# Loading v and z as fp32 through SyncE's queue, with casts by ScalarE and GpSimd, in a fused attention and token-mixing kernel

## The chip, the cores and the metric

The kernel runs on one core of a Trainium2 chip. The time is the device time of one execution in microseconds (us). Of the kernel before, three runs are shown: 773.23, 775.76 and 777.05 us, median 775.76.

Names: PE is TensorE (PEld its weight loads), DVE is VectorE, ACT is ScalarE, POOL is GpSimd, SP is SyncE. The letter q after an engine's name means its instruction queue.

## The reference

All inputs and the output are fp32; u, v have the shape [8, 3200, 256], z has [8, 3200, 64].

```
scores = (1 / 3200) * z @ z.T            # per batch, 3200 x 3200
attn   = max(scores, 0) ** 2
x      = u * (attn @ v)                  # [8, 3200, 256]

wq, wk = x @ w_q, x @ w_k                # [8, 3200, 64]
W      = (1 / 8) * wq @ wk.T             # per batch, 3200 x 3200
out    = max(W @ x, 0) @ w_out           # [8, 3200, 256]
```

## The kernel before

**Tiling.** The 3200 rows of a batch are 25 tiles of 128, in seven groups of columns: six of 512 and one of 128. For every group the kernel makes score tiles (a 128-row tile of z against the group's columns), squares their positive part, and adds the products with v into accumulators. Two score tiles form a pair: they sit in the two halves of the PE array's rows and share one PSUM slot of two banks. There are two such slots.

**Stages of a pair.** `scores` (L263, PE) writes `sc` in PSUM. `first_stage` evicts it as max(4s, 0) into an fp32 tile `g`, on ACT (L286) or DVE (L290). `second_stage` squares it into an fp16 tile `at`, on ACT (L306) or POOL (L308). The pool of `g` has 7 buffers, that of `at` 16. The score matrix is symmetric, so part of the `at` blocks is not made a second time but turned: SP issues a DMA transpose from `at` to `tt` or `ttl` (L330).

**Second product.** `second_product` (L351, PE) multiplies blocks of `at` or `tt` with rows of `v_sb`, the fp16 copy of v, into `acc`. One step of it is two matmuls, on the two halves of the rows. There are 5,000 such steps in all. At the end of half a group, `gate` adds the two accumulators (L368 on ACT or DVE, L369 on DVE) and POOL multiplies by u (L388) into `x_sb`.

**The second layer.** `x_sb` is transposed by DMA (L400), projected to queries and keys (L417, evicted at L431), the keys are transposed by DMA (L436) and doubled by POOL (L448), and heads = keys.T @ x are summed over the groups (L455, L470). When a batch's heads are known, `mix` (L483) and `proj` (L521) give the output of that batch, evicted by ACT (L551) or DVE (L546) and stored by SP (L552). This work of batch b runs inside the loop of batch b + 1.

**Loads.** u comes by SP as fp32 (L174). v and z of the next batch come as DMAs that cast fp32 to fp16 on the way; these are issued by POOL: `load_v` (L150) five times a batch with 5 row tiles each, `load_z` (L156) once a batch. v has two buffers `v_sb`, so the next batch's v is written while this one's is read. z lands in `zn`, and SP transposes it into `zT` in four DMAs (`turn_z`, L163). The first batch's z is loaded as fp32 and cast on three engines (L110, L124); its v comes by casting DMAs of POOL (L113).

**The order.** All engines run in the order in which the Python program writes the instructions; each engine waits in that order for its operands. The order comes from a planner in the program: it keeps a clock for PE, DVE, ACT and POOL, adds a cost for each instruction (`give`), and chooses the engine of an eviction or a square by these clocks. SP's DMAs stand in a list `moves` with a time when they are ready, a time when they are due, SP's issue cost and the time that the DMA queue takes; `send` issues the one that is due first and plans its landing. A block of `tt` is due 4, 9 or 12 us after its square, by the distance of the groups. `at_time` puts an action at a planned time. `lead` is how many steps of the second product the scores are ahead of the even pace. `SPARE`, `BIAS` and `LATE` bend the choice between engines, `MIXES` spaces the output work, and `calm_for` keeps other work away from the end of a half group.

In every batch but the last, `batch_begun` plans the loads of the next: z 6 us after the batch begins, z's transposes 14 us later and on, v at 20, 33, 46, 59 and 72 us. Of these casting DMAs only the landing is planned (`v_at`); nothing on ACT or POOL waits for it.

Of the kernel before, what the change touches and what calls it, by code (L numbers as in the profile page):

```python
# [16 lines left out]
def kernel(  # L17
# [128 lines left out]

    def load_v(b, n0, nn):
        if n0 == 0:
            vs[b] = pv.tile([P, NT, D], FP16, tag="v_sb", name="v_sb")
        nc.gpsimd.dma_start(out=vs[b][:, n0 : n0 + nn, :], in_=rows(v, b)[:, n0 : n0 + nn, :])  # L150

    ztimes = []
    ZTURNS = [(0, 0, 7), (1, 0, 7), (0, 7, 13), (1, 7, 13)]

    def load_z(b):
        nc.gpsimd.dma_start(out=zn[:, 1 : NT + 1, :], in_=rows(z, b))  # L156

# [441 lines left out]
    mixed_at = []  # L599
    MIXES = 10.0  # L600
    MIXES_END = 14.0
# [7 lines left out]
    LANDS = 4.0  # L609
    RING = 2.0  # L610
    SLACK = 1.0

    def at_time(t, fn):
        later.append((t, fn))
# [80 lines left out]
    def squares():  # L695
        while pending and pending[0][0] <= clock[PE] + 0.3:
# [9 lines left out]
            for (b, gi, gj, _, nn, _, _), turn in second_stage(p, g, ways):  # L706
                n = nn * widths[gi] // P
                due = done + {1: 4.0, 2: 9.0}.get(gj - gi, FARDUE)
                out_of[p] = out_of.get(p, 0) + 1
                move(  # L710
                    done + SLACK, due + SLACK, 1.28, 0.21 * n, turn,
                    lambda t, x=(p, b, gi, gj, nn): block_landed(t, *x),
                    lambda x=(b, gi, gj): has_home(*x),
                )
# [17 lines left out]
    def use_keys(b, gi):  # L732
# [17 lines left out]
        if not final:  # L750
            move(
                done + SLACK, done + 10.0, 1.28, 0.21 * n, lambda: turn_keys(b, gi),
                lambda t: at_time(t, lambda: double(b, gi)),
            )
            keyed.append((b, gi))
# [61 lines left out]
    def project_out(b, gi, ps, ready):  # L817
        stores = []
        on_act = max(clock[ACT], ready) + BIAS <= max(clock[DVE], ready) + 0.2
        proj_out(b, gi, ps, [(not on_act, nc.sync, widths[gi] // P)], stores)  # L820
        engine, t = (ACT, 1.0) if on_act else (DVE, 1.23)
        done = give(engine, ready, t if gi < LASTG else 0.3)
        close_slot(done)
        i = len(stored)
        if gi < LASTG:
            stored.append(1e9)

        def landed(t):
            if gi < LASTG:
                stored[i] = t  # L830

        move(done + SLACK, done + 6.0, 0.55, 1.6, stores[0], landed)

    def push(takes):
        give(POOL, clock[PE], 0.6)
        dma_at[0] = max(dma_at[0], clock[PE]) + takes

    Z0 = 24
    ZWAIT, ZDUE, ZSTEP, ZSTEP0 = 14.0, 32.0, 7.0, 5.0
    V0 = 56  # L840
    V1 = 10

    def batch_begun(b, t):
        if b + 1 < B:
            t0 = max(t + 6, Z0)
            at_time(t0, lambda: (load_z(b + 1), push(3.0)))
            step = ZSTEP if b else ZSTEP0
            for i, (_, m0, m1) in enumerate(ZTURNS):
                move(
                    t0 + ZWAIT + step * i, t0 + ZDUE + step * i, 1.28, 0.21 * (m1 - m0),  # L850
                    lambda i=i: turn_z(b + 1, i),
                    lambda t, i=i: z_ready.update({(b + 1, i): t}),
                )
            for i in range(5):
                at = t + 20 + 13 * i if b else V0 + V1 * i
                at_time(at, lambda i=i: v_loaded(b + 1, 5 * i, 5))

    def v_loaded(b, n0, nn):
        load_v(b, n0, nn)
        push(2.5)  # L860
        for n in range(n0, n0 + nn):
            v_at[b, n] = dma_at[0] + 5.0

# [6 lines left out]
    def group_begun(b, gi, t):  # L870
        if gi == 0:
            batch_begun(b, t)
        if gi + 1 < NG:
            move(max(t + 2, clock[POOL] + SLACK), t + 7, 0.55, 1.6, lambda: load_u(b, gi + 1))
        elif b + 1 < B:
            move(max(t + 2, clock[POOL] + SLACK), t + 7, 0.55, 1.6, lambda: load_u(b + 1, 0))

    SPARE = 0.5
    BIAS = 0.2
    XDUE = 5.0  # L880
    XWAIT = 2.0
    LATE = 0.5

    def half_done(b, gi, half):
# [10 lines left out]
        if half == halves(gi)[-1]:  # L895
            n = 8 if widths[gi] == W else 2
            move(
                t + SLACK, t + XDUE, 1.28, 0.21 * n, lambda: turn_x(b, gi),
                lambda t: x_landed(t, b, gi), lambda: len(xTs) < NXT,
# [120 lines left out]
    at_time(V3, lambda: (load_first_v(4, 8), give(POOL, clock[PE], 0.6)))  # L1020
    move(10.0, 14.0, 0.55, 1.6, lambda: load_u(0, 0))
    load_weights()
# [3 lines left out]
    done_acc = 0  # L1026
    lead = 140
    turn_about = False
# [146 lines left out]
```

## Time and profile before

One execution was profiled. It took 773.15 us; its span, from the first instruction to the last, is 770.9 us.

| What | us | share of the span |
|---|---|---|
| Profiled execution, its own time | 773.15 | |
| Its span | 770.9 | |
| PE busy | 761.7 | 99% |
| POOL busy | 591.1 | 77% |
| ACT busy | 561.2 | 73% |
| DVE busy | 510.5 | 66% |
| DMA queue of SP, share of the 16 DMA engines | | 85.0% |
| DMA queue of POOL, share of the 16 DMA engines | | 14.8% |

Issuing a DMA counts as busy on POOL (0.59 us each) but not on SP. Matmul rows overlap, since a matmul starts before the one ahead of it has ended; so the mean of a matmul's row is longer than its step. In rows of groups, the order is: line, engine, operation, output<-inputs, shapes, count, then busy us and mean ns of one, then the idle time before them and what ended it. In rows of one source line the durations are minimum/median/maximum in ns.

### The profile page before, as it was taken

To read this page: it belongs to the slowest core of one execution; us is meant where nothing else is said; L and a number is where in the kernel's file an instruction comes from. 1 tells how busy PE (TensorE), PEld (TensorE's weight loads), DVE (VectorE), ACT (ScalarE), POOL (GpSimd) and SP (SyncE) were. 2 spreads that over 40 slices of the span, in tenths; PEclk is the share of its full clock that TensorE was granted. 3 is DMA by queue.
4 is the path that set the end of the run, shared out by engine and by line. 5 is a ranking of instruction groups with operands and counts; after the bars stand their busy time and mean duration, and the time that the engine had idled before them with its cause. 6 is when DMAs were issued, how large, how long until landed. Compare 5 with 4: busy or idle time off the path is not lost.

```text
span 770.9 us, 28221 instructions
## 1 busy us (share of the span) xinstructions
PE 761.7 (99%) x12408; PEld 678.4 (88%) x12408; DVE 510.5 (66%) x537; ACT 561.2 (73%) x647; POOL 591.1 (77%) x496
## 2 busy tenths in 40 slices
PE   8999999999999999999999999999999999999996
PEld 7889998888898888989889988998889989898884
DVE  6775876675787566765677756765667476675645
ACT  7785876778758678875788677877777676777734
POOL 8796788789687778666778687887878887888740
PEclk9999999999999999999999999999999999999998
DMA  8999999999999999999899999999999998979625
GB/s 199 130 187 182 167 204 173 160 212 194 194 162 189 194 209 190 182 213 203 153 190 162 188 231 163 219 145 160 262 156 192 184 190 211 201 143 203 152 84 191
DMA packets 307114, 141.09 MB, mean 183 GB/s; under 512 B 285744, under 2 KB 288432, under 8 KB 306992
## 3 DMA queue, kind: packets, MB, share of 16 engines
q1 hardware_dynamic: 300224, 123.13, 85.0%
q0 software_dynamic: 6624, 15.98, 14.8%
q8 instruction: 97, 1.59, 0.9%
q14 instruction: 25, 0.20, 0.1%
q10 hardware_dynamic: 144, 0.20, 0.1%
HBM read 59.64 MB, written 26.21 MB: 111 GB/s over the span
## 4 chain that ended last, share of the span: by engine, by line
PE 94%; POOL 2%; DVE 1%; DMA 1%; ACT 1%; issue 1%; POOLq 0%; SPq 0%; DVEq 0%; ACTq 0%
PE acc L351 68%; PE sc L263 13%; PE fo L521 6%; PE qk L417 3%; PE qk L455 2%; POOL at L308 2%; PE mx L483 1%; DMA z<-in_z_dram 1%; POOL x_sb L388 1%; DVE g L290 0%; ACT g L286 0%; DVE fo L546 0%; DMA xT_sb<-x_sb 0%; PE hd L455 0%; ACT at L306 0%
## 5 line engine op out<-in xcount | busy, mean ns | idle before, releaser
L351 PE MATMUL acc<-v_sb,at 64*128 64x256 f16 x7344 | 504.7, 269 | 0.0
L308 POOL TENSOR_TENSOR at<-g 128x1024 f16<-128x1024 f32 (+1 forms) x218 | 402.3, 1859 | 71.6 <-ACT g L286 29.1
L351 PEld LDWEIGHTS <-at 64*128 64x128 f16 x7344 | 407.2, 94 | 48.1 <-issue 4.8
L290 DVE TENSOR_SCALAR g<-sc 128x1024 f32<-128x1024 f32 (+2 forms) x285 | 338.5, 1203 | 122.8 <-PE sc L263 114.3
L306 ACT ACTIVATE at<-g 128x1024 f16<-128x1024 f32 (+2 forms) x255 | 257.2, 1023 | 21.8 <-DVE g L290 17.8
L286 ACT ACTIVATE g<-sc 128x1024 f32<-128x1024 f32 (+2 forms) x186 | 183.2, 989 | 76.8 <-PE sc L263 75.0
L388 POOL TENSOR_TENSOR x_sb<-both,u_sb 128x512 f16<-128x512 f32 (+1 forms) x112 | 135.8, 1217 | 81.6 <-DVE both L369 77.7
L263 PE MATMUL sc<-zT 64*128 64x512 f16 x924 | 188.1, 375 | 1.4 <-DVE g L290 0.6
L351 PE MATMUL acc<-v_sb,tt 64*128 64x256 f16 x2272 | 163.4, 269 | 0.0
L351 PEld LDWEIGHTS <-tt 64*128 64x128 f16 x2272 | 126.2, 94 | 10.3
L369 DVE TENSOR_TENSOR both<-acc,both 128x512 f32<-128x512 f32 (+1 forms) x104 | 69.6, 670 | 21.4 <-ACT both L368 17.0
L263 PEld LDWEIGHTS <-zT 64*128 64x128 f16 x924 | 61.2, 94 | 7.6 <-issue 3.9
L368 ACT COPY both<-acc 128x512 f32<-128x512 f32 (+1 forms) x69 | 39.0, 565 | 38.7 <-PE acc L351 36.1
L546 DVE TENSOR_SCALAR fo<-fo 128x1024 f32<-128x1024 f32 (+1 forms) x28 | 32.4, 1166 | 46.6 <-PE fo L521 46.6
L509 ACT ACTIVATE rt<-mx 128x1024 f16<-128x1024 f32 x39 | 39.9, 1024 | 12.6 <-PE mx L483 12.1
L521 PE MATMUL fo<-wo,rt 128*128 128x256 f16 x386 | 46.6, 273 | 0.5 <-ACT rt L505 0.5
L521 PEld LDWEIGHTS <-rt 128*128 128x128 f16 x386 | 36.2, 98 | 8.4 <-issue 3.6
L431 ACT CAST qk<-qk 128x512 f16<-128x512 f32 (+1 forms) x47 | 25.3, 539 | 24.6 <-PE qk L455 20.0
L368 DVE COPY both<-acc 128x512 f32<-128x512 f32 (+1 forms) x35 | 23.6, 674 | 21.2 <-PE acc L351 19.9
L470 DVE TENSOR_TENSOR ha<-qk,ha 128x512 f32<-128x512 f32 x37 | 25.5, 689 | 14.4 <-ACT qk L431 14.1
L551 ACT ACTIVATE fo<-fo 128x1024 f32<-128x1024 f32 (+2 forms) x23 | 22.5, 978 | 16.5 <-PE fo L521 15.8
L417 PE MATMUL qk<-xT_sb,wqk 64*128 64x256 f16 (+1 forms) x404 | 32.3, 265 | 0.0
(55 smaller groups left out, 282.9 us busy)
## 6 DMA issues: line engine op xcount, KB each, us to landing
u_sb<-in_u_dram SPq DMA_DIRECT2D x48, 512.0 KB, 4.8
out_dram<-fo SPq DMA_DIRECT2D x46, 512.0 KB, 5.1
v_sb<-in_v_dram POOLq DMA_DIRECT2D x35, 320.0 KB, 6.0
zn<-in_z_dram POOLq DMA_DIRECT2D x7, 400.0 KB, 7.8
tt<-at SPq DMA_TRANSPOSE x143, 4.7
u_sb<-in_u_dram SPq DMA_DIRECT2D x8, 128.0 KB, 2.9
out_dram<-fo SPq DMA_DIRECT2D x4, 256.0 KB, 3.3
xT_sb<-x_sb SPq DMA_TRANSPOSE x56, 5.4
```

What stands on the lines that cost most here:

```text
L263: nc.tensor.matmul(out=sc[h][:, 0:gw] if banks else sc[:, h, 0:gw], lhsT=z_cols(b, h, ti * P, P), rhs=z_cols(b, h, gs, gw), start=True, st ...
L286: nc.scalar.activation(out=g[:, hs, 0:w], in_=part, func=RELU, scale=GSCALE)
L290: nc.vector.tensor_scalar(out=g[:, hs, 0:w], in0=part, scalar1=0.0, scalar2=GSCALE, op0=AOP.max, op1=AOP.mult,)
L306: nc.scalar.square(out=out, in_=g[:, hs, 0:w])
L308: nc.gpsimd.tensor_mul(out=out, in0=g[:, hs, 0:w], in1=g[:, hs, 0:w])
L351: nc.tensor.matmul(out=accs[half, r][:, ds((j % 2) * D, D)], lhsT=weights(b, gi, ti, j)[top(r), :], rhs=vs[b][top(r), ti, :], start=(first ...
L368: copy(out=both[:, 0 : n * D], in_=accs[half, 0][:, 0 : n * D])
L369: nc.vector.tensor_add(out=both[:, 0 : n * D], in0=accs[half, 1][:, 0 : n * D], in1=both[:, 0 : n * D])
L388: nc.gpsimd.tensor_mul(out=xs[b, gi][:, 0:n, :, r, :].rearrange("p n c d -> p (n c) d"), in0=both[:, 0 : n * D].rearrange("p (m d) -> p m ...
L417: nc.tensor.matmul(out=ps[:, r, 0 : n * P], lhsT=wqk[top(r), c, :, :].rearrange("p t h -> p (t h)"), rhs=xTs[b, gi][top(r), 0:n, c, :], st ...
L509: nc.scalar.activation(out=out, in_=part, func=RELU)
L521: nc.tensor.matmul(out=banks[r][:, ds(j * D, D)], lhsT=flat[:, ds((dc * n + j) * P, P)], rhs=wo[:, dc, :], start=(dc == 0 and j == 0), sto ...
```

## The change

1. **Loads.** `load_v`, `load_z` and the five-part schedule of v go. In their place a table `PARTS` lists ten loads a batch: z whole, then v in nine parts of 2, 3 or 5 row tiles. Each is a plain fp32 DMA issued by SP (0.45 us of SP in the plan). With the 7 batches that load a next one, 42 DMAs of POOL become 70 of SP.
2. **Staging.** The fp32 data land in parts of the next batch's `v_sb` buffer that hold nothing yet (five of the ten loads; the fourth number in the table is the row tile where the staging begins), or in two small tiles of 3 and 2 row tiles (`pst`). To make room, the pool of `g` goes from 7 buffers to 6. A load that reuses staged space is sent only after the casts that read it are planned to be over.
3. **Casts.** `part_landed` casts a landed part to fp16, three row tiles of v or nine of z at a time, on ACT or POOL by the planner's clocks. That is 13 casts a batch, 91 in all. They are placed `CASTS` = 6.0 us behind the planned landing. z's transposes follow the end of its casts instead of fixed times.
4. **Plan.** Costs and margins change: the issue of a transpose from 1.28 to 1.25 us of SP and from 0.21 n to 0.2 + 0.13 n us of the queue (n blocks), plain loads from 0.55 and 1.6 to 0.45 and 1.7, SP at most 1.5 us ahead of the queue instead of 2.0, the doubling of keys 1 us later, `MIXES` 10 to 14, `SPARE` 0.5 to 0.3, `BIAS` 0.2 to 0, `LATE` 0.5 to 0.3, `lead` 140 to 160. The arithmetic on PE is the same, in another order; which engine evicts, squares or copies what comes out differently.

```diff
-    pg = ctx.enter_context(tc.tile_pool(name="pg", bufs=7))
+    pst = ctx.enter_context(tc.tile_pool(name="pst", bufs=1))
+    pg = ctx.enter_context(tc.tile_pool(name="pg", bufs=6))
...
-    def load_v(b, n0, nn):
-        if n0 == 0:
+    STAGES = (3, 2)
+    PARTS = [
+        (False, 0, 25, 12.5, 0),
+        (True, 0, 3, 6, 0),
+        (True, 3, 5, 15, 1),
+        (True, 8, 2, 11, 2),
+        (True, 10, 3, None, 0),
+        (True, 13, 2, None, 0),
+        (True, 15, 2, 21, 3),
+        (True, 17, 3, None, 5),
+        (True, 20, 2, None, 6),
+        (True, 22, 3, None, 8),
+    ]
+    stage_of = {}
+
+    def load_part(b, i):
+        is_v, n0, nn, slot, _ = PARTS[i]
+        if i == 0:
             vs[b] = pv.tile([P, NT, D], FP16, tag="v_sb", name="v_sb")
-        nc.gpsimd.dma_start(out=vs[b][:, n0 : n0 + nn, :], in_=rows(v, b)[:, n0 : n0 + nn, :])
+        size, what = (D, v) if is_v else (dqk, z)
+        if slot is None:
+            k = STAGES.index(nn)
+            stage = pst.tile([P, nn * D], FP32, tag=f"st{k}", name="st")[:]
+        else:
+            at = int(slot * D)
+            stage = vs[b][:].rearrange("p n d -> p (n d)")[:, at : at + 2 * nn * size].bitcast(FP32)
+        stage_of[b, i] = stage.rearrange("p (n d) -> p n d", d=size)
+        nc.sync.dma_start(out=stage_of[b, i], in_=rows(what, b)[:, n0 : n0 + nn, :])
+
+    def cast_part(b, i, m0, m1, by_act):
+        is_v, n0, _, _, _ = PARTS[i]
+        copy = nc.scalar.copy if by_act else nc.gpsimd.tensor_copy
+        out = vs[b][:, n0 + m0 : n0 + m1, :] if is_v else zn[:, 1 + m0 : 1 + m1, :]
+        copy(out=out, in_=stage_of[b, i][:, m0:m1, :])
...
-    def load_z(b):
-        nc.gpsimd.dma_start(out=zn[:, 1 : NT + 1, :], in_=rows(z, b))
...
-    MIXES = 10.0
+    MIXES = 14.0
...
-    RING = 2.0
+    RING = 1.5
...
-        dma_at[0] = max(dma_at[0], begun) + takes
         sp_at[0] = max(begun + issue, dma_at[0] - RING)
+        dma_at[0] = max(dma_at[0], begun + max(issue, 0.9)) + takes
         if landed:
-            landed(max(sp_at[0], dma_at[0]) + LANDS)
+            landed(dma_at[0] + LANDS)
...
+    Z1 = 6
+    VTIMES = [0, 4, 18, 23, 28, 34, 40, 46, 53, 60]
+    V0 = 0.75
+    CASTS = 6.0
+    KEYS = 1.0
+    ZWAIT, ZDUE, ZSTEP, ZSTEP0 = 1.0, 18.0, 7.0, 5.0
...
+        for i, (is_v, _, nn, _, after) in enumerate(PARTS):
+            at = t0 + VTIMES[i] * (1.0 if b else V0)
+            move(
+                at, at + 8.0, 0.45, 0.2 + 1.5 * nn * (D if is_v else dqk) / 1024,
+                lambda i=i: part_sent(b + 1, i),
+                lambda t, i=i: at_time(t + CASTS, lambda: part_landed(b + 1, i)),
+                lambda i=i, after=after: sent[b + 1] == i and cast[b + 1][0] >= after
+                and (not after or cast[b + 1][1] + SLACK <= clock[PE]),
+            )
...
+    def part_landed(b, i):
+        assert cast[b][0] == i
+        is_v, n0, nn, _, _ = PARTS[i]
+        size, most = (D, 3) if is_v else (dqk, 9)
+        for m0 in range(0, nn, most):
+            m1 = min(nn, m0 + most)
+            n = (m1 - m0) * size
+            a, c = (max(clock[x], clock[PE]) for x in (ACT, POOL))
+            t_act, t_pool = 0.19 + 0.00084 * n, 0.15 + 0.0009 * n
+            by_act = a + SPARE < c and (a + t_act <= shut() + LATE or a + 2.5 < c)
+            cast_part(b, i, m0, m1, by_act)
+            done = give(ACT, clock[PE], t_act) if by_act else give(POOL, clock[PE], t_pool)
+            if is_v:
+                v_at.update({(b, n0 + m): done + 0.3 for m in range(m0, m1)})
...
-    SPARE = 0.5
-    BIAS = 0.2
+    SPARE = 0.3
+    BIAS = 0.0
...
-    LATE = 0.5
+    LATE = 0.3
...
-    lead = 140
+    lead = 160
```

More of the change, by code (lines that the diff above doesn't have):

```diff
@@ L710, in squares @@
                 move(
-                    done + SLACK, due + SLACK, 1.28, 0.21 * n, turn,
+                    done + SLACK, due + SLACK, 1.25, 0.2 + 0.13 * n, turn,
                     lambda t, x=(p, b, gi, gj, nn): block_landed(t, *x),
@@ L830, in landed @@
                 stored[i] = t
[L832 to L836, printed above, removed]
+        move(done + SLACK, done + 6.0, 0.45, 1.7, stores[0], landed)
     Z0 = 24
-    ZWAIT, ZDUE, ZSTEP, ZSTEP0 = 14.0, 32.0, 7.0, 5.0
-    V0 = 56
-    V1 = 10
-    def batch_begun(b, t):
[L844 to L848, printed above, removed]
+    Z1 = 6
@@ new lines, in part_sent @@
+    def part_sent(b, i):
+        sent[b] += 1
+        load_part(b, i)
+    def part_landed(b, i):
[12 more added lines that the diff above has]
+                v_at.update({(b, n0 + m): done + 0.3 for m in range(m0, m1)})
+        cast[b] = [i + 1, done]
+        if not is_v:
+            step = ZSTEP if b > 1 else ZSTEP0
+            for k, (_, m0, m1) in enumerate(ZTURNS):
@@ L849, in batch_begun @@
                 move(
-                    t0 + ZWAIT + step * i, t0 + ZDUE + step * i, 1.28, 0.21 * (m1 - m0),
-                    lambda i=i: turn_z(b + 1, i),
-                    lambda t, i=i: z_ready.update({(b + 1, i): t}),
-                )
[L854 to L862, printed above, removed]
+                    done + ZWAIT + step * k, done + ZDUE + step * k, 1.25, 0.2 + 0.13 * (m1 - m0),
@@ L873, in group_begun @@
         if gi + 1 < NG:
-            move(max(t + 2, clock[POOL] + SLACK), t + 7, 0.55, 1.6, lambda: load_u(b, gi + 1))
+            move(max(t + 2, clock[POOL] + SLACK), t + 7, 0.45, 1.7, lambda: load_u(b, gi + 1))
         elif b + 1 < B:
-            move(max(t + 2, clock[POOL] + SLACK), t + 7, 0.55, 1.6, lambda: load_u(b + 1, 0))
-    SPARE = 0.5
-    BIAS = 0.2
+            move(max(t + 2, clock[POOL] + SLACK), t + 7, 0.45, 1.7, lambda: load_u(b + 1, 0))
+    SPARE = 0.3
+    BIAS = 0.0
     XDUE = 5.0
     XWAIT = 2.0
-    LATE = 0.5
+    LATE = 0.3
     def half_done(b, gi, half):
@@ L1020 @@
     at_time(V3, lambda: (load_first_v(4, 8), give(POOL, clock[PE], 0.6)))
-    move(10.0, 14.0, 0.55, 1.6, lambda: load_u(0, 0))
+    move(10.0, 14.0, 0.45, 1.7, lambda: load_u(0, 0))
     load_weights()
```

15 lines of the change are left out of this document (12 added, 3 removed).

## The prediction

> **What bounds the kernel now.** I read the busy shares first, then the table of engine times by stage, then who makes TensorE wait, then the chain of waits.
>
> ```profile
> PE 761.7 (99%) x12408; PEld 678.4 (88%) x12408; DVE 510.5 (66%) x537; ACT 561.2 (73%) x647; POOL 591.1 (77%) x496
> ...
> 0.00:10.00 10.00, 8.29 (x82) 6.37 (x84) 5.54 (x10) 5.80 (x9) 6.59 (x15) 1.00 0.81 209
> 10.00:25.00 15.00, 14.68 (x229) 12.24 (x227) 11.79 (x11) 12.45 (x15) 14.73 (x9) 1.00 0.66 149
> 25.00:50.00 25.00, 24.43 (x405) 21.83 (x402) 17.84 (x18) 18.67 (x20) 20.73 (x17) 1.00 1.08 165
> 50.00:97.00 47.00, 46.91 (x801) 44.05 (x796) 34.15 (x38) 34.76 (x39) 35.76 (x32) 1.00 1.22 177
> 97.00:193.00 96.00, 96.00 (x1592) 85.22 (x1587) 63.83 (x69) 72.60 (x81) 81.83 (x69) 1.00 1.03 188
> ...
> 481.00:577.00 96.00, 95.89 (x1580) 85.65 (x1578) 59.70 (x63) 75.69 (x85) 77.84 (x64) 1.00 1.07 189
> ...
> 673.00:740.00 67.00, 67.00 (x1096) 60.14 (x1094) 43.97 (x47) 49.73 (x59) 53.56 (x42) 1.00 0.76 153
> 740.00:771.00 31.00, 24.54 (x332) 18.91 (x328) 15.17 (x21) 9.84 (x21) 5.18 (x4) 0.93 0.45 162
> ```
>
> After the first row, each line is a stretch, its length, then busy time and count for PE, PEld, DVE, ACT and POOL, then the granted clock and DMA's share. PE is idle 1.71 + 0.32 + 0.57 = 2.6 us up to 50 us, 0.09 in the next stretch, 0.11 in the stretch at 481, and nothing in the others up to 740; the end has 6.46. The 96 us stages hold 1592 and 1580 matmuls, so the pace hardly differs between them. The busy rows can hide a short pause, so the waits and the chain are needed too.
>
> ```profile
> PE sc L263 <- DVE g L290: 0.6, 2, 0.4
> PE sc L263 <- ACT g L286: 0.3, 1, 0.3
> PE 94%; POOL 2%; DVE 1%; DMA 1%; ACT 1%; issue 1%; POOLq 0%; SPq 0%; DVEq 0%; ACTq 0%
> 10.00 10.30 POOL at L308 x6
> 30.46 4.37 PE acc L351 x80
> 128.01 1.20 PE acc L351 x22
> ```
>
> The third number of a wait row is the longest wait. PE's waits are tenths of a microsecond, and 94% of the chain is PE. The only long leg elsewhere is at 10 to 20 us, six GpSimd squares. (The last two rows are single legs of it: start, length, count.) An acc matmul costs 4.37 / 80 = 54.6 ns, so a step of the planner (two of them) is 0.109 us. Neither loading v nor z appears as something PE waits for. A change of loads can therefore win little in this execution.
>
> **The change, part by part.** *PE* keeps all its matmuls; six head matmuls move from a separate bank to the merged one, at the same price. This part is 0.
>
> *Issues leave GpSimd, casts come.* The program as built has 91 casts where 42 casting DMAs stood. On ScalarE: 18 of 512 columns, 23 of 768, 10 of 576, 5 of 448. On GpSimd: 17, 12, 4 and 2.
>
> ```profile
> L150 POOL DMA_DIRECT2D v_sb<-in_v_dram x35 | 20.7, 591 | 0.0
> L156 POOL DMA_DIRECT2D zn<-in_z_dram x7 | 4.1, 591 | 0.0
> L124 ACT CAST zd<-z 128x512 f16<-128x512 f32 x1 | 0.6, 619 | 1.8 <-DMA z<-in_z_dram 1.8
> L124 ACT CAST zd<-z 128x256 f16<-128x256 f32 x1 | 0.4, 404 | 1.2 <-DMA z<-in_z_dram 1.2
> L124 POOL CAST zd<-z 128x512 f16<-128x512 f32 x1 | 0.6, 609 | 0.9 <-DMA z<-in_z_dram 0.9
> L124 POOL CAST zd<-z 128x384 f16<-128x384 f32 x1 | 0.5, 503 | 1.4 <-DMA z<-in_z_dram 1.4
> L308 POOL TENSOR_TENSOR at<-g 128x1024 f16<-128x1024 f32 x211 | 396.5, 1893 | 70.0 <-ACT g L286 29.1 <-DVE g L290 29.0 <-issue 9.6
> L306 ACT ACTIVATE at<-g 128x1024 f16<-128x1024 f32 x240 | 250.8, 1056 | 21.8 <-DVE g L290 17.8
> L290 DVE TENSOR_SCALAR g<-sc 128x1024 f32<-128x1024 f32 x278 | 335.2, 1221 | 121.8 <-PE sc L263 113.3 <-POOL at L308 3.3 <-ACT g L286 1.8
> L286 ACT ACTIVATE g<-sc 128x1024 f32<-128x1024 f32 x175 | 178.8, 1023 | 75.0 <-PE sc L263 73.2 <-POOL kx L448 0.9 <-POOL hs L477 0.6
> L368 ACT COPY both<-acc 128x512 f32<-128x512 f32 x63 | 36.8, 584 | 34.3 <-PE acc L351 31.7 <-PE sc L263 1.1 <-PE hd L455 1.0
> L431 ACT CAST qk<-qk 128x512 f16<-128x512 f32 x40 | 23.4, 586 | 23.0 <-PE qk L455 18.5 <-PE qk L417 4.2
> L551 ACT ACTIVATE fo<-fo 128x1024 f32<-128x1024 f32 x21 | 21.5, 1024 | 15.6 <-PE fo L521 14.8 <-DMA u_sb<-in_u_dram 0.8
> ```
>
> ScalarE's slope is (619 - 404) / 256 = 0.84 ns a column, so 768 columns cost 0.83 us, 576 0.67, 448 0.57: 18 x 0.62 + 23 x 0.83 + 10 x 0.67 + 5 x 0.57 = 39.8 us. GpSimd's slope is (609 - 503) / 128 = 0.83, giving 17 x 0.61 + 12 x 0.82 + 4 x 0.66 + 2 x 0.56 = 24.0 us, against 42 x 0.591 = 24.8 us of issues removed: even. The planner also moves squares: 20 fewer on ScalarE (-21.1 us), 18 more whole ones on GpSimd (+34.1 us). ScalarE takes 16 result copies (+16.4) and 8 evictions (+8.2) from VectorE and gives it 21 accumulator copies (-12.3) and 8 qk copies (-4.7): +7.6. ScalarE thus goes to 561 + 40 - 21 + 8 = 588 us (76%), GpSimd to 591 - 1 + 34 = 624 us (81%). Both stay below the span, so I cost this at nothing; the cover is the 147 us of idle time that GpSimd keeps, and the squares made ahead of PE. The planner's lead rises from 140 to 160 steps: 160 x 0.109 = 17.4 us against 15.3. If that cover is gone, PE next waits at a score pair for a PSUM slot. One g buffer fewer (7 to 6) works against it. With 278 + 175 evictions in 771 us a pair comes every 1.7 us, so six buffers still hold 10 us, above an eviction (1.2), a square ahead (1.9) and its own (1.9). Bounds: 0, or an eviction that stands behind one cast and is late by its 0.83 us in each batch; I take 0, as PE's score waits are tenths.
>
> *SyncE and the DMA queue.* SyncE gets 70 more loads.
>
> ```profile
> L330 SPq DMA_TRANSPOSE tt<-at x143: 1231/1354/5576, 17.1 to 713.4; - x143
> L330 SPq DMA_TRANSPOSE ttl<-at x48: 1193/1262/2715, 26.4 to 723.4; - x48
> L400 SPq DMA_TRANSPOSE xT_sb<-x_sb x56: 1190/1295/4657, 35.7 to 754.5; - x56
> L436 SPq DMA_TRANSPOSE kx<-qk x53: 1182/1233/2294, 50.2 to 733.7; - x53
> L163 SPq DMA_TRANSPOSE zT<-zn x28: 1215/1297/4448, 41.1 to 626.3; - x28
> L174 SPq DMA_DIRECT2D u_sb<-in_u_dram x56: 327/529/1814, 5.0 to 738.3; - x56
> q0 software_dynamic: 6624, 15.98, 14.8%
> u_sb<-in_u_dram SPq DMA_DIRECT2D x48, 512.0 KB, 4.8
> v_sb<-in_v_dram POOLq DMA_DIRECT2D x35, 320.0 KB, 6.0
> tt<-at SPq DMA_TRANSPOSE x143, 4.7
> u_sb<-in_u_dram SPq DMA_DIRECT2D x8, 128.0 KB, 2.9
> SPq L330 <- ACT g L286: 42.7, 17, 9.9
> ```
>
> By the medians the transposes take 143 x 1.35 + 48 x 1.26 + 56 x 1.30 + 53 x 1.23 + 28 x 1.30 = 428 us of SyncE, and its 114 loads and stores, all priced as u's 0.53, 60: 488 us, 63%. Seventy more at 0.53 add 37 us: 68%. It stays free a third of the time. On the DMA engines the bytes read are the same (a 320 KB load of fp16 already reads 640 KB of fp32) and the bytes stored double. Lower bound: no change. Upper bound: the 14.8% share, nine tenths of it for these loads, doubles, +13 points. I take a value near the lower, as the 512 KB u load lands in 4.8 us and the v load with 640 KB read in 6.0. But the loads now stand in the transposes' own queue. From the two u rows, (4.8 - 2.9) us / 384 KB = 4.9 ns a KB, a 640 KB part holds the queue 3.2 us, and z's 800 KB 4.0 us. A transpose behind it lands at 4.7 + 3.2 = 7.9 us; the blocks are wanted the planner's due 4 to 12 us after the square, and the new plan knows the load stands there. Cost 0; the other bound is 3.2 us less the two groups of 22 acc matmuls (1.2 us each) that PE has before it needs a new score pair, 0.8 us a late block.
>
> The Trainium skill, "DMA: Bandwidth & Descriptors", section on queues, rings and completion order, says each DMA engine serves its queues in turn, packet by packet. By it the old loads shared with the transposes while the new ones go wholly before them, which speaks against the change; if that were not hidden the sum would be that of the queue rival below, while the row of 4.7 us with PE's waits of tenths says that several microseconds are hidden today.
>
> *Casts that wait.* A cast waits in ScalarE's or GpSimd's order for its landing; behind it stand evictions and squares. It is placed 6 us behind the planned landing. Nothing in this trace shows such a wait, so bounds: 0, or the 9.9 us that SyncE was once held, less 6, which is 3.9 us. I take 0, as the 42.7 us in 17 waits are 2.5 on the mean, inside the 6.
>
> *The retuned plan.* The planned landing of an eight-block transpose moves from 1.68 + 4 us after the issue to 1.25 + 1.24 + 4, or 0.8 us later; keys get 1 us more. This removes pauses where data come late.
>
> **The sum.** The profiled execution took 773.15 us (span 770.9 and 2.25 around it); the three runs' median, 775.76, is 2.6 above it, the fastest, 773.23, level with it. So the program can run without those 2.6 us. Whether later planning brings it there every time no row shows: bounds 0 and -2.6, and as every margin grows I take all of it, being nearest to the execution whose rows I have. At 10 to 50 us PE's idle 0.89 us lies on the leg of GpSimd squares; the built order gives ScalarE two more half squares among its first eleven squares, so I take -0.7 (bounds +1 and -0.9). The idle 0.2 between 50 and 740 goes. The end has the same order from the last product on: 0. Against the profiled execution: 773.15 - 0.7 - 0.2 = 772.25; from the median, 775.76 - 2.6 - 0.9 = 772.26. Forecast 772.3, 0.45% faster.
>
> **Rivals.** *No gain:* the 2.6 us are of the chip and not of waits, the loads being hidden anyway. For it: PE has almost no wait on DMA. Then 775.76 - 0.9 = about 775.
>
> *Late landings (slower):* a load is held on SyncE for more than the 6 us; its cast holds ScalarE 3.9 us; both PSUM slots run out after two groups of acc matmuls (2 x 1.2 us), and PE stops 1.5 us. Once in each of seven batches: +10.5 on 772.3, 783. For it: the 9.9 us wait; against it: the mean of 2.5. It decides from a landing over 6 us behind plan.
>
> *The one queue (slower):* parts push transposes back by 3.2 us, and SyncE's extra 37 us fall in bursts with u loads and stores. For it: SyncE at 68% and the landing of up to 7.9 us; against it: no PE wait on a transpose of the loop today. If two of a batch's ten parts make a late block: 7 x 2 x 0.8 = +11.2, 783.5. It decides from (779.6 - 772.3) / 7 = 1.0 us a batch.
>
> **How the numbers follow.** Gain 0.66, no gain 0.12, late landings 0.10, the queue 0.12. About 0.5% is what a measurement can tell from no change: below 771.9 is faster, above 779.6 slower. The forecast stands close to the first bound, and pauses hidden in busy rows could bring it to 769: of its 0.66 I put 0.42 below and 0.24 within. With the no-gain case, within is 0.36; the two slower ones give slower 0.22. The range is 769 to 782: downwards the hidden pauses, upwards most of the slower cases. The likeliest case alone has 769 to 775.
>
> **What would show it.** PE's idle time from 50 to 740 us still under 1 us, matmuls per 96 us near 1590: the middle unchanged. ScalarE's wait on v's or z's landing near zero: the 6 us suffice; microseconds there, with score pairs waiting on ScalarE, would be the late landings. Transposes landing in over 8 us with PE waiting on tt or kx would be the queue. PE idle in 10 to 50 us above 0.9 would prove the start wrong. Three runs within 2 us of the profiled execution would support the 2.6 us, runs spread over 4 us again would refute it.

## The result, and the profile after

The changed kernel took 787.71 us (median of 6 runs, 783.07 to 790.69), the kernel before, beside it on the same chip, 775.29 us (6 runs, 773.19 to 780.51). The ratio is 1.0149, with a 95% interval of 1.0101 to 1.0196. The forecast was 772.3 us and the range 769 to 782: wrong in sign and outside the range. The profiled execution of after took 784.85 us, its span is 783.1 us, 12.2 more than before's 770.9.

The page of after: busy shares, the queue of SyncE and the chain of waits. The casting queue's 14.8% went to SyncE's.

```profile
PE 763.5 (97%) x12408; PEld 665.2 (85%) x12408; DVE 506.8 (65%) x547; ACT 576.7 (74%) x679; POOL 623.2 (80%) x506
...
q1 hardware_dynamic: 310304, 151.80, 97.0%
...
PE 80%; DMA 6%; POOL 6%; DVE 3%; issue 2%; ACT 2%; SPq 1%; POOLq 0%; DVEq 0%; ACTq 0%
```

PE was busy 1.8 us longer than before and idle 783.1 - 763.5 = 19.6 us instead of 9.2: of the 12.2 us of span, 10.4 are idle time of PE. DMA has entered the chain with 6% (before 1%), and POOL's share rose from 2% to 6%. The engine times by stage (columns as in the prediction) say where:

```profile
0.00:10.00 10.00, 7.86 (x74) 5.70 (x76) 5.36 (x10) 4.75 (x8) 5.62 (x15) 1.00 0.83 212
10.00:25.00 15.00, 13.59 (x210) 11.16 (x211) 10.78 (x10) 14.43 (x17) 14.98 (x11) 1.00 0.65 138
25.00:50.00 25.00, 24.86 (x415) 22.41 (x413) 18.97 (x20) 20.77 (x24) 21.73 (x18) 1.00 0.97 198
50.00:97.00 47.00, 42.43 (x719) 38.41 (x716) 31.35 (x34) 31.98 (x39) 36.09 (x30) 1.00 1.08 196
97.00:193.00 96.00, 95.51 (x1564) 81.22 (x1560) 64.35 (x69) 72.02 (x85) 75.93 (x62) 1.00 1.01 207
...
385.00:481.00 96.00, 93.92 (x1542) 82.32 (x1540) 62.41 (x68) 72.21 (x86) 77.57 (x63) 1.00 1.04 206
481.00:577.00 96.00, 94.05 (x1549) 83.30 (x1546) 60.95 (x66) 71.02 (x82) 77.09 (x66) 1.00 1.03 206
577.00:673.00 96.00, 96.00 (x1588) 84.80 (x1584) 62.79 (x69) 74.13 (x87) 81.28 (x66) 1.00 1.05 206
```

Up to 50 us PE is idle 2.14 + 1.41 + 0.14 = 3.7 us, 1.1 more than before. From 50 to 740 us it loses 4.57 + 0.49 + 2.08 + 1.95 in the stages shown and 0.36 in the others, 9.45 us where before had 0.2. The stage that loses nothing holds 1588 matmuls, like before's 1580 to 1592, so the pace itself did not change. The waits of PE and POOL name what it is:

```profile
PE qk L445 <- DMA xT_sb<-x_sb: 9.3, 7, 2.5
...
POOL kx L476 <- DMA kx<-qk: 30.0, 13, 5.9
...
ACT v_sb L181 <- DMA st<-in_v_dram: 1.0, 1, 1.0
```

The same row of POOL in the kernel before, where PE waits at no projection of the loop:

```profile
POOL kx L448 <- DMA kx<-qk: 2.2, 2, 2.0
```

Seven times PE stands at a projection because the transposed x has not landed, 9.3 us in all; GpSimd waits 30.0 us for transposed keys (before 2.2). The casts, which the prediction worried about, waited once, for 1.0 us.

One wait in full, the third transposed x. The last product that fills this x ended at 56.07 + 1.28 = 57.35 us. That row, then SyncE's, then PE's projection, in the timeline (start, us, instruction):

```profile
56.07 1.28 POOL L416 TENSOR_TENSOR x_sb<-both,u_sb 128x512 f16<-128x512 f32 x1
...
56.86 1.43 SPq L191 DMA_TRANSPOSE zT<-zn  x1
58.39 0.53 SPq L175 DMA_DIRECT2D v_sb<-in_v_dram  x1
58.97 0.42 SPq L175 DMA_DIRECT2D st<-in_v_dram  x1
59.49 2.01 SPq L358 DMA_TRANSPOSE tt<-at  x1
61.54 0.58 SPq L175 DMA_DIRECT2D st<-in_v_dram  x1
62.21 2.72 SPq L358 DMA_TRANSPOSE tt<-at  x2
65.03 0.54 SPq L202 DMA_DIRECT2D u_sb<-in_u_dram  x1
65.62 1.23 SPq L428 DMA_TRANSPOSE xT_sb<-x_sb  x1
...
72.78 0.61 PE L445 MATMUL qk<-xT_sb,wqk 64*128 64x256 f16 x8 [2.06 <-DMA xT_sb<-x_sb]
```

SyncE works without a gap of more than a tenth, and the transpose is issued 8.3 us after its data are there. The chain has the same piece (`65.62 7.12 DMA xT_sb<-x_sb`), and PE stops for 2.06 us. The same x in the kernel before:

```profile
59.19 1.28 SPq L330 DMA_TRANSPOSE ttl<-at  x1
60.56 0.54 SPq L174 DMA_DIRECT2D u_sb<-in_u_dram  x1
61.15 2.85 SPq L400 DMA_TRANSPOSE xT_sb<-x_sb  x1
64.11 8.10 SPq L330 DMA_TRANSPOSE tt<-at  x3
72.26 1.26 SPq L436 DMA_TRANSPOSE kx<-qk  x1
73.56 1.28 SPq L163 DMA_TRANSPOSE zT<-zn  x1
...
71.45 0.62 PE L417 MATMUL qk<-xT_sb,wqk 64*128 64x256 f16 x8
```

SyncE is just as full here: three transposes take 8.10 us, 2.7 each. But it sends the x transpose ahead of keys and of z, and the projection comes when the data are there. The planner's own times, taken from the program as it is built, show why (us; by the end of this x's product, the kernel itself is there 1.2 us ahead of plan in before, 0.4 behind it in after and 1.1 behind it in e14, which is an experiment below):

```
third x         sent: plan, trace    projected: plan, trace
before              62.7, 61.15             72.4, 71.45
after               59.3, 65.62             69.8, 72.78
e14_late_use        61.2, 71.53             73.1, 78.39
```

Before, the plan believed SyncE later than it was; after, it believes it 6 us earlier. So two theories go to the experiments. *The plan:* the smaller planned cost of a DMA transpose (1.25 us instead of 1.68 for eight blocks) makes the plan run ahead of SyncE. *The loads:* 70 loads more in SyncE's list, or the casts, cost the time whatever the plan believes.

### The profile page after: what moved, and what is told of

Read it like the earlier page. It is cut to its first block, busy times and chain, and to the rows that moved or that the text cites. A ratio compares the mean times of both kernels' runs of the same rounds, so it can differ in the third digit from the quotient of the medians.

```text
span 783.1 us, 28419 instructions
## 1 busy us (share of the span) xinstructions
PE 763.5 (97%) x12408; PEld 665.2 (85%) x12408; DVE 506.8 (65%) x547; ACT 576.7 (74%) x679; POOL 623.2 (80%) x506
## 4 chain that ended last, share of the span: by engine, by line
PE 80%; DMA 6%; POOL 6%; DVE 3%; issue 2%; ACT 2%; SPq 1%; POOLq 0%; DVEq 0%; ACTq 0%
PE acc L379 58%; PE sc L291 10%; DMA xT_sb<-x_sb 6%; PE fo L549 5%; POOL at L336 4%; PE qk L445 3%; PE qk L483 2%; DVE g L318 2%; PE mx L511 1%; POOL x_sb L416 1%; DMA z<-in_z_dram 1%; ACT g L314 1%; ACT at L334 0%; SPq L464 0%; DVE fo L574 0%
## 5 line engine op out<-in xcount | busy, mean ns | idle before, releaser
L336 POOL TENSOR_TENSOR at<-g 128x1024 f16<-128x1024 f32 (+1 forms) x234 | 435.8, 1875 | 53.8 <-DVE g L318 45.2
L379 PEld LDWEIGHTS <-at 64*128 64x128 f16 x7344 | 396.0, 94 | 56.9 <-issue 4.6
L318 DVE TENSOR_SCALAR g<-sc 128x1024 f32<-128x1024 f32 (+1 forms) x279 | 330.9, 1199 | 156.2 <-PE sc L291 144.9
L334 ACT ACTIVATE at<-g 128x1024 f16<-128x1024 f32 (+2 forms) x241 | 238.5, 1008 | 14.2 <-DVE g L318 11.2
L379 PE MATMUL acc<-v_sb,tt 64*128 64x256 f16 x2272 | 152.9, 269 | 0.0
L397 DVE TENSOR_TENSOR both<-acc,both 128x512 f32<-128x512 f32 (+1 forms) x104 | 69.8, 671 | 19.3 <-ACT both L396 13.4
L396 DVE COPY both<-acc 128x512 f32<-128x512 f32 (+1 forms) x56 | 38.1, 680 | 44.1 <-PE acc L379 43.7
L579 ACT ACTIVATE fo<-fo 128x1024 f32<-128x1024 f32 (+2 forms) x39 | 37.1, 994 | 19.6 <-PE fo L549 18.8
L396 ACT COPY both<-acc 128x512 f32<-128x512 f32 (+1 forms) x48 | 26.8, 559 | 31.8 <-PE acc L379 22.1
L476 POOL COPY kx<-kx 128x128 f16<-128x128 f16 (+1 forms) x99 | 25.5, 287 | 30.0 <-DMA kx<-qk 30.0
L445 PEld LDWEIGHTS <-wqk 64*128 64x128 f16 x416 | 21.5, 94 | 15.1 <-DMA xT_sb<-x_sb 11.2
```

The source lines that it names most:

```text
L318: nc.vector.tensor_scalar(out=g[:, hs, 0:w], in0=part, scalar1=0.0, scalar2=GSCALE, op0=AOP.max, op1=AOP.mult,)
L334: nc.scalar.square(out=out, in_=g[:, hs, 0:w])
L336: nc.gpsimd.tensor_mul(out=out, in0=g[:, hs, 0:w], in1=g[:, hs, 0:w])
L379: nc.tensor.matmul(out=accs[half, r][:, ds((j % 2) * D, D)], lhsT=weights(b, gi, ti, j)[top(r), :], rhs=vs[b][top(r), ti, :], start=(first ...
L396: copy(out=both[:, 0 : n * D], in_=accs[half, 0][:, 0 : n * D])
L397: nc.vector.tensor_add(out=both[:, 0 : n * D], in0=accs[half, 1][:, 0 : n * D], in1=both[:, 0 : n * D])
```

## The experiments

All are compared with the kernel before, run beside them; its medians were 774.8 to 775.8 us. The diffs are shortened: a changed number is shown once and stands for every place where it occurs. The first number of a planned DMA is SyncE's issue, the second the queue's time (n blocks of a transpose).

**e1_truth: after, with SyncE's share of each DMA made dearer.**

```diff
-  1.25, 0.2 + 0.13 * n
+  1.75, 0.2 + 0.13 * n
-  0.45, 1.7
+  0.6, 1.7
```

> The changed kernel, with the planner's cost of SyncE's issues raised to what the trace of the changed kernel shows (a transpose 1.25 to 1.75 us, a plain DMA 0.45 to 0.6). Plan theory (the plan charges SyncE too little, so the projections are placed ahead of their transposed x): TensorE's wait on xT falls from 9.3 us to under 2, time 774 to 778. Queue theory (70 more DMAs are too much work for SyncE's queue, however they are planned): the wait on xT or another wait stays, 783 to 790.

Measured: 793.12 us (791.74 to 793.63), ratio 1.0204 (1.0145 to 1.0263). PE's waits in it:

```profile
PE sc L291 <- DVE g L318: 6.6, 11, 1.2
PE qk L445 <- DVE g L318: 1.6, 3, 0.7
```

The wait for the transposed x is gone, as the theory of the plan has it, but the time is a miss for it and lies above the queue theory's range too: the planned end itself moves out by more than 20 us, and PE now waits most for score slots. Charging too much costs as well.

**e2_xwait: after, each projection 4 us later behind its planned landing.**

```diff
-    XWAIT = 2.0
+    XWAIT = 6.0
```

> The changed kernel, with XWAIT 2 to 6: the projections wait 4 us longer after the planned landing of x, nothing else of the plan's costs is changed. Plan theory: the wait on xT falls under 2 us and the time to 775 to 779. Queue theory: the lateness grows with the backlog (up to 12 us behind plan), so waits move to other places; 782 to 790.

Measured: 780.47 us (778.05 to 786.54), ratio 1.0062 (1.0022 to 1.0103); the wait at the projections falls to 4.2 us in two. Over half of the loss goes with a margin alone, without touching a load or a charge; but time and wait both miss the plan theory's numbers (775 to 779 us, under 2 us).

**e3_costs_alone: before, with all of after's DMA costs,** its rule for `send` and `RING` 1.5; no load moves.

```diff
-    RING = 2.0
+    RING = 1.5
...
-        dma_at[0] = max(dma_at[0], begun) + takes
         sp_at[0] = max(begun + issue, dma_at[0] - RING)
+        dma_at[0] = max(dma_at[0], begun + max(issue, 0.9)) + takes
         if landed:
-            landed(max(sp_at[0], dma_at[0]) + LANDS)
+            landed(dma_at[0] + LANDS)
...
-  1.28, 0.21 * n
+  1.25, 0.2 + 0.13 * n
-  0.55, 1.6
+  0.45, 1.7
```

> The kernel before, its loads and casts as they were, with the changed kernel's planner costs alone (issue and queue costs of DMAs, RING, the planned landing). Plan theory: TensorE begins to wait on xT here too, 3 to 10 us, time 778 to 786. Queue theory: without the 70 loads SyncE keeps up, time within 2 us of before, 773 to 777.

**e4_loads_oldcosts: after, with before's costs, rule and `RING`;** the loads and casts stay. Its diff against after is that of e3 backwards, and 0.55 us of issue for the new loads.

> The changed kernel, with the planner costs of the kernel before (1.28 and 0.21 n for a transpose, 0.55 and 1.6 for a plain DMA, RING 2.0, the landing as before). Plan theory: the old costs overcharge plain DMAs, so the plan leaves room; time 773 to 778, wait on xT under 2 us. Queue theory: 782 to 790, since the loads are still in SyncE's queue.

Measured: e3 791.64 us (ratio 1.0187, 1.0122 to 1.0253), e4 775.23 us (0.9995, 0.9967 to 1.0023). The waits of e3:

```profile
PE qk L417 <- DMA xT_sb<-x_sb: 9.5, 6, 4.3
...
POOL kx L448 <- DMA kx<-qk: 31.4, 12, 5.1
```

These are after's two waits, 9.3 and 30.0, in a kernel that loads v and z by GpSimd as ever. And e4, with all the new loads, waits at no projection in the loop. The costs carry the loss, the loads do not. (e3 even loses more than the 778 to 786 us that the plan theory gave.)

**e5_choices_alone: before, with the numbers that bend the planner's choices.**

```diff
+    MIXES = 14.0
+    SPARE = 0.3
+    BIAS = 0.0
+    LATE = 0.3
+    lead = 160
```

> The kernel before with SPARE, BIAS, LATE, MIXES and lead of the changed kernel, its loads and DMA costs as they were. If the costs of DMAs alone do the harm: 773 to 778, TensorE's wait on xT under 1 us. If these choices have a part in it: over 779.

Measured: 777.43 us (773.69 to 780.78), 1.0022 (0.9991 to 1.0053): no measurable part.

**e6_takes_back: after, only the transposes' charge taken back;** **e7_send_back: after, only the rule for `send`, `RING` and the planned landing taken back.**

```diff
-  1.25, 0.2 + 0.13 * n
+  1.28, 0.21 * n
```

That is e6; e7 against after is the first part of e3's diff backwards.

> The changed kernel with the old cost of a transpose alone (issue 1.28, queue 0.21 n: 1.68 us for eight blocks instead of 1.24). Theory that the sustained cost of a transpose was set too low: wait on xT under 2 us, 774 to 779. Theory that the new way of sending (SyncE allowed further ahead of the queue) is what misleads the plan: 783 to 790.

> The changed kernel with the old rule of sending alone (RING 2.0 and the queue's time added before SyncE's limit, the old planned landing), the new costs per DMA kept. Theory of the transpose's cost: still 783 or more, wait on xT 5 us or more. Theory of the sending rule: 774 to 779.

Measured: e6 777.39 us (nine of its ten executions 776.43 to 779.22; the tenth, 4025 us, stands apart), 1.0032 (1.0019 to 1.0046), no wait for a transposed x, though 0.3% over before remain; e7 792.58 us, 1.0217 (1.0183 to 1.025), with that wait at 7.6 us in four. Of the retuned DMA numbers it is the transposes' charge.

**e8_loads_alone: before's planner in every number, with after's loads, staging, casts and six buffers of g.** Against after it is e4 and, beside it, the choices of e5 and `KEYS` taken back.

> The changed kernel with every planner number of the kernel before (costs, sending rule, SPARE, BIAS, LATE, MIXES, lead, no extra wait for keys); only loads, staging, casts and the six g buffers are new. If loads and casts cost nothing by themselves: 773 to 778, ratio 0.997 to 1.004. If the queue or the casts cost something that the other choices hid: 779 to 784.

Measured: 781.57 us (781.04 to 783.33), 1.0089 (1.0065 to 1.0113), 6 us over before, as the second theory has it, although all stages from 50 us on are nearly full. The loss lies at one place, in PE's timeline and in 2 us windows (granted clock behind the fifth count):

```profile
39.46 2.01 PE L379 MATMUL acc<-v_sb,at 64*128 64x256 f16 x33 [0.53 <-DVE both L397]
44.58 0.39 PE L445 MATMUL qk<-xT_sb,wqk 64*128 64x256 f16 x1 [3.10 <-POOL wqk L233]
```

```profile
46.00:48.00 2.00, 2.00 (x20) 1.45 (x18) 0.69 (x1) 0.00 (x0) 0.00 (x0) 0.50 0.69 154
48.00:50.00 2.00, 2.00 (x22) 1.45 (x20) 1.23 (x1) 0.73 (x1) 0.00 (x0) 0.50 0.66 110
...
52.00:54.00 2.00, 2.00 (x37) 1.74 (x35) 1.30 (x2) 1.75 (x2) 0.47 (x1) 1.00 1.30 260
```

The first projection waits 3.10 us for its weights, which GpSimd casts late (`cast_weights`, planned at 40 us), and then PE runs at half its clock until 51 us (0.50 in both windows, 1.00 in the third): 20 and 22 matmuls in 2 us instead of 37. If that is all, casting the weights earlier must bring it back, which e11 tries.

**e9_transpose_cost: before, with the transposes' charge changed** and nothing else.

```diff
-  1.28, 0.21 * n
+  1.25, 0.2 + 0.13 * n
```

> The kernel of before with one thing changed: the planner's charge for a DMA transpose, from 0.21 us a block of queue time (1.68 us for eight blocks, 1.28 of issue) to 0.2 + 0.13 a block (1.24, and 1.25 of issue), at the four places where one is planned. No load moves. Theory A (this charge alone makes the loss, with or without the loads): 783 to 792 us, TensorE waiting 5 us or more at the projections for the transposed x. Theory B (it harms only together with the other retuned numbers, such as the send rule or the landing of plain transfers): 773 to 778 us, that wait under 1 us.

Measured: 789.03 us (787.76 to 790.14), 1.0178 (1.0147 to 1.0208). PE waits in it `PE qk L417 <- DMA xT_sb<-x_sb: 7.5, 8, 1.7`. Two more waits, 1.9 us in all, are for the projections' weights. One charge in the planner, on the untouched kernel, costs 789.03 - 775.60 = 13.4 us, as much as the whole change. Theory A.

**e11_loads_weights: e8 with the weights cast earlier.**

```diff
-        at_time(40.0, cast_weights)
+        at_time(35.0, cast_weights)
```

> The kernel of the loads alone (v and z as fp32 by SyncE, every planner number of before) with the projections' weights cast at 35 us of the planner's time instead of 40. Theory A (loads and casts cost nothing by themselves; its 6 us over before are the one wait of 3.5 us for those weights and the half clock behind it): 774 to 778 us, the stretch 25 to 50 us at 24 us of TensorE work or more, no slice of the page there under 9 of clock. Theory B (the loads cost by themselves): still 780 us or more.

Measured: 776.82 us (775.09 to 778.79), 1.0015 (0.9991 to 1.0039); the stretch 25 to 50 us holds 24.33 us of PE's work (20.61 in e8). Loads, staging, casts and the missing buffer of g cost nothing that can be measured; what they did in e8 was to bring GpSimd to the weights later (at 43.77 us, in before at 41.35). Theory A.

**e12_takes_mid: after, with a charge between the two.**

```diff
-  1.25, 0.2 + 0.13 * n
+  1.28, 0.19 * n
```

> The kernel after the change with the charge for a DMA transpose between the two: 1.28 us of issue and 0.19 us a block (1.52 for eight blocks; after has 1.24 and 787.7 us, the charge of before 1.68 gave 777.4 us). Theory A (the loss grows with how far the charge falls short of what the queue gives): 777 to 783 us, wait for the transposed x between 0 and 5 us. Theory B (a chance effect of one order of work): anywhere, also over 787 us.

Measured: 774.61 us (772.57 to 781.15), 0.9989 (0.9958 to 1.0019). The loss is gone already here, more than was expected of half the way, so theory A misses its range: the loss does not grow evenly with the charge. Its profile, of the slowest of its ten executions, still waits 5.0 us in three. The kernel equals before and does not beat it.

**e10_probe: before, with useless DMAs behind its last store,** which price SyncE's queue.

```diff
+    for _ in range(28):
+        probe_turn()    # nc.sync.dma_start_transpose, eight blocks
+    for _ in range(14):
+        probe_turn()
+        probe_load()    # nc.sync.dma_start, 512 KB of u
+    for _ in range(12):
+        probe_load()
```

> The kernel of before with work of no use added behind its last store: 28 DMA transposes of eight blocks back to back on SyncE, then 14 pairs of such a transpose and a 512 KB load of u, then 12 loads. It prices the queue. Theory A (issue sets the pace; what lengthens a transpose in the kernel is the traffic and the backlog around it): 1.25 to 1.4 us from transpose to transpose, 1.9 to 2.1 a pair, 0.6 to 0.7 a load as long as their landings keep up. Theory B (the queue itself sustains no more than one per 1.7 to 1.9 us): 1.7 us or more from transpose to transpose, 3 us or more a pair. The time of the whole is that of before plus these, 850 to 950 us.

It took 863.0 us in its one execution. SyncE's timeline of the added part:

```profile
767.77 39.38 SPq L1158 DMA_TRANSPOSE probe_t<-probe_src  x29
807.47 0.34 SPq L1162 DMA_DIRECT2D probe_v<-in_u_dram  x1
807.87 1.24 SPq L1158 DMA_TRANSPOSE probe_t<-probe_src  x1
...
838.21 1.71 SPq L1158 DMA_TRANSPOSE probe_t<-probe_src  x1
839.96 12.26 SPq L1162 DMA_DIRECT2D probe_v<-in_u_dram  x13
```

29 transposes of eight blocks take (807.47 - 767.77) / 29 = 1.37 us each. From 807.87 to 838.21 there are 12 pairs, 2.53 us each; less some 0.6 for the load's step, a transpose between loads takes 1.9. So the first part agrees with theory A, the pairs lie between the two, and a load alone took 12.26 / 13 = 0.94, over what was expected. The charge of 1.25 is below even the 1.37 of a queue with nothing else in it; before's 1.68 is not.

Two more runs asked by which way the charge harms. **e13_early_use: before, each projection 3 us earlier**, no charge changed. **e14_late_use: e9, with the margin given back by hand.**

```diff
e13, against before
-    XWAIT = 2.0
+    XWAIT = -1.0
e14, against e9
-    XWAIT = 2.0
+    XWAIT = 5.0
-                lambda t: at_time(t, lambda: double(b, gi)),
+                lambda t: at_time(t + 3.0, lambda: double(b, gi)),
```

> The kernel of before with one number changed: XWAIT, the planner's pause between the planned landing of a transposed x and the projection that reads it, from 2 us to -1. Every charge and load is as before. It puts the projections 3 us earlier without touching what the plan believes of SyncE (in before the projection starts 15.6 us after GpSimd's product on the median, in after 12.6). Theory A (the loss is projections placed ahead of their data): 780 to 790 us, TensorE waiting 4 us or more at the projections for the transposed x. Theory B (the loss comes from what the smaller charge does to the order in SyncE's list): 773 to 778 us, that wait under 1 us.

> The kernel of before with the smaller charge for a transpose (that alone gave 789.0 us) and the two uses put 3 us later by hand: XWAIT from 2 to 5 us and the doubling of the keys 3 us behind its planned landing. Theory A (the charge harms through the margin of what reads the transposes): 773 to 779 us, both waits near zero. Theory B (it harms through the order in SyncE's list): still 784 us or more.

Measured: e13 780.68 us (780.1 to 781.47), 1.0079 (1.0057 to 1.0101); e14 785.48 us (783.21 to 786.0), 1.0135 (1.0112 to 1.0158). Their waits at the projections, e13's first:

```profile
PE qk L417 <- POOL wqk L205: 2.3, 2, 1.8
...
PE qk L417 <- DMA xT_sb<-x_sb: 1.3, 1, 1.3
```

```profile
PE qk L417 <- DMA xT_sb<-x_sb: 7.3, 2, 3.8
...
POOL kx L448 <- DMA kx<-qk: 3.6, 2, 3.4
```

Early use harms by itself (e13 lies in theory A's range), both waits being projections placed ahead of what they read; but the x's share is 1.3 us and the weights' 2.3, so theory A's 4 us of waiting for x is missed. In e14 the many small waits are gone, GpSimd's for keys fall from 21.1 us to 3.6, and PE loses nothing from 193 to 740 us, where e9 loses 6.4. But two waits before 193 us, 7.3 us in all, keep it at 785, which is theory B's number; by hand only 3.5 of e9's 13.4 us came back. The table above has the third x of e14: sent 10 us behind plan. A margin of 3 us covers the mean and not such a stretch. So both ways stay: the margin explains the late loop (e2, e14), and what is left in e14 fits the order of SyncE's list, which is only argued: no run changed the order alone.

## Why the prediction was wrong, point by point

**The failed step is "The retuned plan ... This removes pauses where data come late."** The prediction read the planned cost of a transpose as a measure that a retuning had brought closer to the chip, and looked only at the planned landing of one transpose in an empty queue (0.8 us later). In a full queue it is the charge per transpose that counts, and that fell from 1.68 to 1.25. The sum took it for granted that "every margin grows"; the margin of what reads the transposes shrank. Nothing in the sum stood for that: its term was 0 or a gain, and it measured +13.4 us (e9).

What it does can be counted over all 56 transposed x of each trace. The table gives PE's wait for x in all (0.2 is at the end, behind the loop), the median from the end of GpSimd's product to the projection, and by how much SyncE sends its DMAs behind plan on the mean, with PE's own delay taken off:

```
kernel                 charge, 8 blocks   time     wait for x   product to projection   SyncE behind plan
before                 1.68               775.3    0.2          15.6                    -1.8
e6_takes_back          1.68               777.4    0            15.7                    -1.2
e4_loads_oldcosts      1.68               775.2    0.2          13.4                    +0.1
e12_takes_mid          1.52               774.6    5.0          14.0                    +1.4
after                  1.25               787.7    9.3          12.6                    +2.0
e9_transpose_cost      1.25               789.0    7.5          11.3                    +1.0
e3_costs_alone         1.25               791.6    9.5          12.3                    +1.6
e7_send_back           1.25               792.6    7.6          11.3                    +1.7
e2_xwait               1.25               780.5    4.2          16.3                    +2.8
e14_late_use           1.25               785.5    7.3          14.6                    +1.0
```

The transposes themselves did not get slower: x lands 5.0 us behind its issue (median, before 5.4), and the issue stands 2.6 us behind the product (before 2.0). The projections came 3 us earlier. Neither of the last two columns sorts the runs alone (e4 projects 13.4 us behind the product without a wait, because its SyncE keeps to the plan); every run of the table with long waits has SyncE 1 us or more behind it. What sorts them is the margin itself, from the landing of an x to its projection, over the 54 of the loop: its median is 5.0 to 8.4 us in the three kernels of the table with 1.68, and no projection comes within 1 us of its landing; in the four with 1.25 and nothing given back (after, e9, e3, e7) it is 3.1 to 4.2 us, and 6 to 11 projections start within 0.3 us of the landing, that is, as soon as they can. With margin given back by hand it is 7.4 us in e2 and 6.9 in e14, with two and three such projections; e12 stands between (4.9 us, four). Before's plan had a margin that it did not know of: SyncE was ahead of it.

**SyncE "stays free a third of the time": wrong, and it hid the first.** The prediction took medians of a skewed duration. The row of before that it quoted has 1231/1354/5576 ns for `tt`; the timeline shows 8.10 us for three. Another stretch, from before's mid-loop:

```profile
401.00 6.83 SPq L330 DMA_TRANSPOSE tt<-at  x2
407.92 1.40 SPq L436 DMA_TRANSPOSE kx<-qk  x1
409.41 1.26 SPq L330 DMA_TRANSPOSE tt<-at  x1
410.76 0.53 SPq L174 DMA_DIRECT2D u_sb<-in_u_dram  x1
411.38 1.73 SPq L163 DMA_TRANSPOSE zT<-zn  x1
413.21 3.99 SPq L330 DMA_TRANSPOSE tt<-at  x1
417.25 2.22 SPq L400 DMA_TRANSPOSE xT_sb<-x_sb  x1
419.56 3.92 SPq L330 DMA_TRANSPOSE tt<-at  x2
423.54 1.29 SPq L163 DMA_TRANSPOSE zT<-zn  x1
```

Ten transposes take 22.64 us, 2.3 each, and nothing but a tenth lies between two instructions. Summed over the whole trace from 50 to 740 us, the 308 transposes of before have a mean of 1.69 us against a median of 1.29, and SyncE is taken for 88% of the time (576 us of issues and 30 us in gaps under 0.2 us), after for 92%. The DMA engines' share in the stage rows from 25 to 577 us, 1.03 to 1.22, pointed to it in the prediction's own first fence. With 63% believed, a plan that charges less looked harmless; on a queue that is nearly full it is not.

**The loads, the casts, the engines: right.** Costed at 0, measured 0 (e4 0.9995, e11 1.0015). ACT and POOL were forecast at 588 and 624 us and came at 577 and 623; the casts' 6 us sufficed but for one wait of 1.0 us. The rival of late landings did not happen. The rival of the one queue named the right resource, and nearly the size (783.5) by luck, since it laid it to the 70 loads and to `tt`; it was the plan, and x and keys. The rule that was weighed there, from the Trainium skill, "DMA: Bandwidth & Descriptors", section "Queues, rings and completion order", spoke against loads in the transposes' own queue; the times of e4 and e11 show no cost from it. That loads can stand ahead of a transpose, as the prediction drew from the rule, the trace after does show: three v parts and a u load are issued before the third x.

**The 2.6 us of the median: wrong as a gain.** Later planning should have brought every run to the profiled one. It did not: the runs of before go from 772.96 to 782.41 us, those of e12, as fast, from 772.57 to 781.15. So the spread stays whatever the plan; the last section has a part of it.

**The start and the end.** At 10 to 50 us 0.7 us less idle time was forecast; it was 1.55 instead of 0.89. PE's named waits there are for evictions, 0.7 us by ACT and 0.7 by DVE (before 0.3 and 0.6), and ACT, which the forecast gave more work, was busy 14.43 of the 15 us from 10 to 25, before 12.45; that this is the cause is not shown. The end costs 6.5 us as before.

## What to carry to other kernels

Where a planner orders the work, its cost for an operation is a part of the kernel: lowering one towards what the operation takes alone removes margin from everything that waits for it, so try that number alone before it goes in with another change. Price a queue by its timeline in a full stretch, or by sums, and not by medians; and where it is full, ask who reads its results, and how much later than the data.

## What the runs showed of the hardware that was not expected

- **A pause of a few us costs twice.** In e8 a wait of 3.10 us left PE at a clock of 0.50 for some 6 us; in e14 one of 3.77 us did so for about 3. Shorter pauses did it too: one of 2.70 us in e2 (0.50 from 91 to 93 us), and in e9 one of 1.36 us with another of 0.53 right behind it (0.55 and 0.60 in the two windows from 46 to 50 us). After's waits, up to 2.51 us, leave its stages at 1.00. So the length of one pause does not decide it alone. The Trainium skill, "TensorE: Matmul & The Clock Gate", section "Part 1: The HAM clock gate", gives a half clock after an idle window of about 3.4 us and full speed again after as long a busy one; the half agrees, but shorter pauses sufficed here, and e8's way back was longer.
- **One of the opening loads has two speeds.** The last of the four loads of the first z, 256 KB, lands in 4.6 to 4.9 us in seven of the sixteen profiles, in 6.5 to 6.7 in eight others, and in 5.6 in after's, without regard to the kernel. In the slower case PE does 60 to 64 matmuls in the first 10 us, instead of 80 to 82, and waits 1.4 to 2.6 us for z's casts; in seven of the eight the granted clock from 10 to 25 us then reads 0.84 to 0.93, in all other profiles 1.00. Up to 25 us before does 311 matmuls and e13, with the slow load, 269: at 54.6 ns each that is 2.3 us, an estimate of what it adds to the spread between runs of one kernel, and near the 2.6 us that the prediction gave to the plan.
- **A DMA transpose has no one price.** Eight blocks take 1.37 us with nothing else running in the program, 1.9 between 512 KB loads, 1.69 on the mean of the loop, smaller ones included, and 2.3 in the full stretch above. Why such a stretch is dearer than the pairs was not tried.
